# A fused attention and expert kernel: the second stage's loads asked earlier on the SP queue, the last additions in another order, the last pair in halves

## The chip, the cores and the metric

The kernel runs on one core of a Trainium2 chip. The metric is the time of one execution on the device in microseconds. Engines: PE is TensorE (matmuls), DVE is VectorE, ACT is ScalarE, POOL is GpSimd; SP is the engine that only issues DMAs here. DMAs are also issued from ACT and from POOL, each with its own queue.

## The reference

The reference computes a sparse attention and feeds its result to a mixture of experts.

- Attention: 8 batches, 8 heads, 512 local and 32 global tokens, head size 64. Global queries see all keys; local queries see the global keys and the local keys within 32 positions. Softmax in both cases. The result x has 4352 rows (8 x 544) of 512 numbers.
- Routing: `P = exp(x @ w_gate - max)` for 8 experts; then eight rounds in which the rows and then the columns are divided by their sums and everything is multiplied by N / E.
- Experts: for each of 8 experts `h = max(x @ w1[e], 0)` (512 to 1024), `y = h @ w2[e]` (1024 to 512), and `out += P[:, e] * y`.

The output is 4352 x 512 numbers in fp32.

## The kernel before

**First stage (0 to about 405 us).** Attention for all batches, the logits, and, as filling work for TensorE, the first expert layer of experts 0 to 3, whose results h are written to DRAM (`hd`). The transposed x is kept in DRAM too (`xd`), as are the fp16 copies of w1 for experts 4 to 7 (`w1d`). At the end of the stage the routing weights go to DRAM (`pd`).

**Second stage (405 to 1054 us): units and pairs.** Its work is cut into 72 units. Tokens stand in nine groups: eight of 512 local tokens, one per batch, and a last one of 256 global tokens. Each group has eight units, one per expert, in the order 4, 0, 5, 1, 6, 2, 7, 3. An even unit uses an expert of 4 to 7, whose first layer is computed here; the odd unit behind it uses an expert of 0 to 3, whose h is loaded. The loop over units (lines 922 to 961) is an order written out by hand, and every engine follows it in its own queue. A "block" here is an even unit with the odd one behind it, counted by the even unit: block 66 is units 66 and 67.

What one block i does:

- SP loads the routing weights of two units as rows spread over all partitions (`load_pb`, tile pb, 256 KB each, 128 KB in the last group), once per group the next group's x (`load_x`, tile xg), the h of unit i + 3 (`load_h`, 1 MB, 512 KB in the last group), and in the odd half the w1 of unit i + 6 (`load_w1`, tile w1s, 1 MB).
- VectorE forms the sums of unit i + 1 (`sums`, line 672 through the helper `tt`), multiplies x by the weights of unit i + 4 (`scale_x`, tile xs), multiplies the loaded h of unit i + 3 by its weights (`scale_h`), and in the odd half forms the sums of unit i + 2.
- TensorE computes the first layer of unit i + 2 (`l1`, line 734; ACT moves it out with Relu, line 736) between the products of unit i (`product`, line 777), and then the products of unit i + 1.

**The second layer in seven products.** h @ w2 is done by a scheme of Strassen's kind: seven products q = 1 to 7 of half-size blocks, from h itself (q 3, 4, 6, 7) and from the sums s (q 1, 2, 5), with weight combinations made beforehand (`prep_w2c`, done on VectorE; three of the experts are still loaded and prepared during the first blocks). Products 1 to 5 are gathered over the whole group in PSUM tiles that stay (`ps_fix`, m1 to m5). Products 6 and 7 are gathered over one block only, in tiles of a rotating PSUM pool with three buffers (`ps_rot`, tag r), which the first layer's results (ph) use as well. At a block's end `add` (lines 782 to 793) moves pm of q 6 and 7 into the output tile o; at the end of a group it also moves m1 to m5. A moved product is one or two instructions, on VectorE (line 793) or as a copy on ACT (line 791). When a group closes, `store` (line 796) issues its store on SP, 1 MB.

**Buffers.** pb, xs and xg have two buffers each, w1s two, h four. A load waits on SP until the last reader of its buffer is done. A pb takes the buffer that was freed first, so in each pair one waits for the last `scale_x` and the other for the last `scale_h`.

**The order on SP.** In the odd half: w1s, then the store if the group closes. In the next even half: pb, pb, xg if due, h. SP works through this strictly in order, so what stands behind a waiting DMA waits too.

**The end.** The last unit (71) is not done in seven products. `last_pair` (lines 798 to 817) computes the second layer of 256 tokens in two pieces of 128 rows, in a PSUM tile of 512 columns each, the right half of the columns first. VectorE adds a piece to o in one instruction (line 813), and the piece's four batches are stored by four DMAs of 64 KB, from SP, ACT and POOL. The additions of unit 70, which close the last group, are written after all its products, in the order 6, 7, 3, 4, 5, 2, 1.

Of the kernel before, what the change touches and what calls it, by code (L numbers as in the profile page):

```python
# [10 lines left out]
FP32 = mybir.dt.float32  # L11
AF = mybir.ActivationFunctionType
ALU = mybir.AluOpType
# [10 lines left out]
def kernel(  # L24
# [13 lines left out]
    nc = tc.nc  # L38
# [3 lines left out]
    D, E = moe_w_gate.shape  # L42
    F = moe_w1.shape[2]
    P = 128
# [45 lines left out]
    with tc.tile_pool(name="att_c", bufs=1) as att_c, \  # L90
# [144 lines left out]
        for a in range(2):  # L235
            r = slice(HB * a, HB * (a + 1))
# [336 lines left out]
        for s in range(HP, NU + 1):  # L573
            slot = s
            b, hp = divmod(s, HP)
# [87 lines left out]
    HF, HD = FT // 2, D // 2  # L663
# [7 lines left out]
    def tt(out, in0, in1, op):  # L671
        nc.vector.tensor_tensor(out=out, in0=in0, in1=in1, op=op)  # L672

    def prep_w2c(e):
        w = w2c[e]
        for o, a, b, op in ((0, 1, 4, ALU.add), (5, 1, 2, ALU.add), (6, 3, 4, ALU.add),
                            (2, 2, 4, ALU.subtract), (3, 3, 1, ALU.subtract)):
            tt(w[:, :, o], w[:, :, a], w[:, :, b], op)
# [8 lines left out]
    def load_w1(i):  # L687
        if i < NUN:
            w1s[i] = wpool.tile([P, DP, F], FP16, tag="w1e", name="w1s")
            nc.sync.dma_start(out=w1s[i], in_=w1d[units[i][1] - NL])  # L690

    def load_pb(i):
        if i < NUN:
            m, e = units[i]
            c0, n = groups[m]
            pbs[i] = xsp.tile([P, 512], FP32, tag="pb", name="pb")
            nc.sync.dma_start(out=pbs[i][:, 0:n], in_=pd[e, c0 : c0 + n].partition_broadcast(P))

    def load_x(m):
        if m <= B:  # L700
            xgs[m] = xsp.tile([P, DP, groups[m][1]], FP16, tag="xg", name="xg")
            nc.sync.dma_start(out=xgs[m], in_=xd[m])

    def scale_x(i):
        if i < NUN:
            m = units[i][0]
            n = groups[m][1]
            xss[i] = xsp.tile([P, DP, 512], FP16, tag="xs", name="xs")
            tt(xss[i][:, :, 0:n], xgs[m],
               pbs.pop(i)[:, 0:n].unsqueeze(1).to_broadcast([P, DP, n]), ALU.mult)  # L710

    def alloc_h(i):
        if i < NUN:
            hs[i] = hpool.tile([P, FT, groups[units[i][0]][1]], FP16, tag="hT", name="h")

    def load_h(i):
        if i < NUN:
            m, e = units[i]
            alloc_h(i)
            nc.sync.dma_start(out=hs[i], in_=hd[e][m])  # L720

    def scale_h(i):
        if i < NUN:
            n = groups[units[i][0]][1]
            h = hs[i]
            tt(h, h, pbs.pop(i)[:, 0:n].unsqueeze(1).to_broadcast([P, FT, n]), ALU.mult)

    def l1(i, fm, pool, tag):
        if i >= NUN:
            return  # L730
        n = groups[units[i][0]][1]
        ph = pool.tile([P, 512], FP32, tag=tag, name="ph")
        for dk in range(DP):
            nc.tensor.matmul(ph[:, 0:n], w1s[i][:, dk, P * fm : P * (fm + 1)], xss[i][:, dk, 0:n],  # L734
                             start=(dk == 0), stop=(dk == DP - 1))
        nc.scalar.activation(out=hs[i][:, fm, 0:n], in_=ph[:, 0:n], func=AF.Relu)  # L736

    def sums(i):
        if i >= NUN - 1:
            return  # L740
        n = groups[units[i][0]][1]
        t1, t2 = slice(0, n // 2), slice(n // 2, n)
        h = hs[i]
        s = ss[i] = (wpool.tile([P, 3, HF, 256], FP16, tag="w2e", name="s", bufs=1) if i % 2 else
                     wr.tile([P, 3, HF, 256], FP16, tag="s", name="s"))
        lo, hi = h[:, 0:HF], h[:, HF:FT]
        tt(s[:, 0:2, :, 0 : n // 2], lo[:, :, 0:n].rearrange("p k (a t) -> p a k t", a=2),
           hi[:, :, 0:n].rearrange("p k (a t) -> p a k t", a=2), ALU.add)
        tt(s[:, 2, :, 0 : n // 2], lo[:, :, t1], hi[:, :, t2], ALU.add)
        tt(lo[:, :, t2], lo[:, :, t2], lo[:, :, t1], ALU.subtract)  # L750
        tt(hi[:, :, t1], hi[:, :, t1], hi[:, :, t2], ALU.subtract)
# [5 lines left out]
    def closes(i):  # L757
        m, e = units[i]
        return e == (ORDER[-1] if m < B else ORDER[-2])
# [22 lines left out]
    def add(i, q, pm):  # L782
        m, e = units[i]
        nt = groups[m][1] // P // 2
        if m not in os_:
            os_[m] = ypool.tile([P, NJ, D], FP32, tag="y", name="o")
        for j, (r, d, sg) in enumerate(QUARTER[q]):
            o = os_[m][:, nt * r : nt * (r + 1), HD * d : HD * (d + 1)]
            p = pm[:, 0 : HD * nt].rearrange("p (t d) -> p t d", d=HD)
            if (q >= 6 and e == ORDER[1]) or (q in (3, 4) and j == 0):  # L790
                nc.scalar.mul(o, p, 1.0 / float(E))  # L791
            else:
                nc.vector.scalar_tensor_tensor(out=o, in0=p, scalar=sg / float(E), in1=o, op0=ALU.mult, op1=ALU.add)  # L793

    def store(m):
        nc.sync.dma_start(out=out[S * m + Sg : S * (m + 1)].rearrange("(c p) d -> p c d", p=P), in_=os_[m])

    def last_pair(i):
        m, e = units[i]
        o, h, w = os_[m], hs[i], w2c[e]  # L800
        n = groups[m][1]
        lo, hi = h[:, 0:HF, 0:n], h[:, HF:FT, 0:n]
        s = ss[i]
        for c in range(n // P):
            q = slice(P * c, P * (c + 1))
            pm = ps_rot.tile([P, 512], FP32, tag="r", name="pm")
            for d, terms in ((1, ((lo, 2), (s, 4))), (0, ((hi, 3), (s, 1)))):
                for t, (a, wi) in enumerate(terms):
                    for k in range(HF):
                        nc.tensor.matmul(pm[:, HD * d : HD * (d + 1)], a[:, k, q], w[:, k, wi, :],  # L810
                                         start=(d == 1 and t == 0 and k == 0),
                                         stop=(t == 1 and k == HF - 1), skip_group_check=True)
            nc.vector.scalar_tensor_tensor(out=o[:, c, :], in0=pm, scalar=1.0 / float(E), in1=o[:, c, :],  # L813
                                           op0=ALU.mult, op1=ALU.add)
            for b in range(4 * c, 4 * c + 4):
                eng = {3: nc.gpsimd, 7: nc.sync}.get(b, (nc.sync, nc.scalar)[c])
                eng.dma_start(out=out[S * b : S * b + Sg, :], in_=o[W * (b % 4) : W * (b % 4 + 1), c, :])  # L817

    fac = float(E) / float(NTOK)
# [90 lines left out]
    for fm in range(FT):  # L910
        pool, tag = cyc[fm % 2]
# [4 lines left out]
    load_w1(4)  # L916
    sums(0)
    scale_h(1)
    pss.close()
    ps_rot = ctx.enter_context(tc.tile_pool(name="ps_rot", bufs=3, space=PSUM, reuse_waits="tile"))  # L920
    ps_fix = ctx.enter_context(tc.tile_pool(name="ps_fix", bufs=1, space=PSUM, reuse_waits="tile"))
    for i, (m, e) in enumerate(units):
        if i == NUN - 1:
            last_pair(i)
        elif i % 2 == 0:
            alloc_h(i + 2)
            load_pb(i + 3)
            load_pb(i + 4)
            if (i + 4) % E == 0:
                load_x((i + 4) // E)  # L930
            load_h(i + 3)
            if i + 2 < NUN:
                sums(i + 1)
            else:
                n = groups[m][1]
                h = hs[i + 1]
                s = ss[i + 1] = wpool.tile([P, HF, n], FP16, tag="w2e", name="sl", bufs=1)
                tt(s, h[:, 0:HF, 0:n], h[:, HF:FT, 0:n], ALU.add)
            scale_x(i + 4)
            if m == 0:  # L940
                for e in {2: (2,), 4: (7,), 6: (3,)}.get(i, ()):
                    prep_w2c(e)
            scale_h(i + 3)
            for fm in range(3):
                l1(i + 2, fm, ps_rot, "r")
            for q, fm in ((3, 3), (4, 4), (5, 5), (2, 6), (1, 7), (6, None), (7, None)):
                product(i, q)
                if fm is not None:
                    l1(i + 2, fm, ps_rot, "r")
            if closes(i):  # L950
                for q in (6, 7, 3, 4, 5, 2, 1):
                    add(i, q, fixed[q])
        else:
            load_w1(i + 5)
            sums(i + 1)
            for q in (6, 7, 3, 4, 5, 2, 1):
                product(i, q)
                if q >= 6 or closes(i):
                    add(i, q, fixed[q])
            if closes(i):  # L960
                store(m)
# [31 lines left out]
```

## Time and profile before

| | |
|---|---|
| median of 3 runs | 1059.76 us (1059.38 to 1062.28) |
| the profiled execution | 1060.91 us |
| its span, first to last instruction | 1059.1 us |
| granted TensorE clock, mean | 0.996 |
| PE busy | 1024.0 us (97%) |
| DVE busy | 809.6 us (76%) |
| ACT busy | 489.1 us (46%) |
| POOL busy | 132.0 us (12%) |
| DMA | 190.82 MB, mean 180 GB/s |

A time line of the profile reads: start in us, duration in us, engine, line of the kernel, operation, what it writes and reads, the shape, how many instructions are merged into the line (x), and in brackets how long the engine stood idle before it and what ended that. SPq and ACTq are DMAs being issued on these engines. A line of waits reads: who waited (engine, tile, line), for whom, us in total, how many times, the longest. Matmuls overlap one another, so a line of x4 that says 0.60 us occupies TensorE until the next line starts. Times of single DMA packets (their size, start and landing) come from the same trace.

### The profile page before, as it was taken

The numbers are of one execution on the slowest core, as the hardware profiler recorded it, in microseconds if no ns is written. First come the engines' busy times: TensorE is split into PE (matmuls) and PEld (weight loads), VectorE is DVE, ScalarE is ACT, GpSimd is POOL, SyncE is SP. The second block draws the span as 40 slices with busy tenths as digits, with TensorE's granted clock in tenths as the row PEclk, the third lists the DMA queues.
The fourth block names the chain that finished last, engine by engine and source line by source line (L and its number), as shares of the span: only waits on it lengthen the run. The fifth ranks groups of instructions, "written<-read, shape, count | busy, mean of one in ns | idle before, by whom it ended". The sixth has DMA issues, their size and how long they took to land.

```text
span 1059.1 us, 21691 instructions
## 1 busy us (share of the span) xinstructions
PE 1024.0 (97%) x8854; PEld 698.6 (66%) x8854; DVE 809.6 (76%) x1464; ACT 489.1 (46%) x1248; POOL 132.0 (12%) x216
## 2 busy tenths in 40 slices
PE   7799999999999999999999999999999999999997
PEld 4455555555555466677777777777777777777786
DVE  8577777777775767997878777778787678668766
ACT  7678888787886674222323223223233132232231
POOL 7341423413313002000000000000000000000000
PEclk9899999999999999999999999999999999999999
DMA  9887588997946999835436346436535535436251
GB/s 267 189 208 210 106 265 195 220 241 153 255 130 177 269 283 302 246 104 189 165 139 197 123 140 199 140 120 199 170 115 177 211 97 186 180 128 181 106 176 49
DMA packets 97331, 190.82 MB, mean 180 GB/s; under 512 B 33424, under 2 KB 63584, under 8 KB 84432
## 3 DMA queue, kind: packets, MB, share of 16 engines
q1 hardware_dynamic: 54208, 159.61, 44.4%
q0 software_dynamic: 40464, 20.26, 14.7%
q10 hardware_dynamic: 2560, 9.57, 2.3%
q8 instruction: 69, 1.13, 0.4%
q14 instruction: 30, 0.25, 0.1%
HBM read 157.11 MB, written 53.62 MB: 199 GB/s over the span
## 4 chain that ended last, share of the span: by engine, by line
issue 63%; PE 21%; ACT 7%; DVE 5%; DMA 2%; POOL 1%; SPq 0%; ACTq 0%; POOLq 0%
PE ph L466 14%; ACT Pu L309 4%; DVE Pu L346 2%; ACT hT L469 1%; PE ptw L357 1%; ACT qbd L283 1%; DMA vraw<-in_v_l_dram 1%; DMA f<-in_q_l_dram 1%; DMA kgf<-in_k_g_dram 1%; PE pt L273 1%; PE ph L734 1%; PE po L378 1%; DVE m L409 1%; PE sc L299 1%; PE pt L426 1%
## 5 line engine op out<-in xcount | busy, mean ns | idle before, releaser
L736 ACT ACTIVATE h<-ph 128x512 f16<-128x512 f32 (+1 forms) x288 | 164.8, 573 | 408.4 <-PE ph L734 398.5
L734 PE MATMUL ph<-xs,w1s 128*128 128x512 f16 (+1 forms) x1152 | 269.6, 367 | 4.4 <-DVE o L793 2.9
L466 PE MATMUL ph<-xT,w1e 128*128 128x512 f16 (+1 forms) x1152 | 256.1, 367 | 0.2
L777 PEld LDWEIGHTS <-h 128*128 128x128 f16 x2160 | 211.4, 98 | 44.3
L777 PE MATMUL m<-w2c,s 128*128 128x256 f16 x1620 | 199.9, 273 | 0.0
L672 DVE TENSOR_TENSOR s<-h 128x1024 f16<-128x1024 f16 (+2 forms) x142 | 123.9, 914 | 86.3 <-PE m L777 43.3
L777 PEld LDWEIGHTS <-s 128*128 128x128 f16 x1620 | 158.5, 98 | 38.2
L734 PEld LDWEIGHTS <-w1s 128*128 128x128 f16 x1152 | 112.6, 98 | 87.6 <-issue 5.1
L466 PEld LDWEIGHTS <-w1e 128*128 128x128 f16 x1152 | 105.2, 98 | 95.8 <-issue 3.0
L672 DVE TENSOR_TENSOR h<-h,pb 128x4096 f16<-128x4096 f16 (+1 forms) x36 | 150.6, 4183 | 3.9 <-DMA h<-hd 3.4
L777 PE MATMUL m<-w2c,h 128*128 128x256 f16 x1080 | 135.2, 273 | 0.0
L469 ACT ACTIVATE hT<-ph 128x512 f16<-128x512 f32 (+1 forms) x191 | 103.6, 558 | 46.4 <-PE ph L466 45.1
L777 PE MATMUL pm<-w2c,h 128*128 128x256 f16 x1080 | 123.8, 273 | 0.0
L672 DVE TENSOR_TENSOR xs<-xg,pb 128x2048 f16<-128x2048 f16 (+1 forms) x36 | 78.1, 2169 | 53.4 <-DMA pb<-pd 47.2
L309 ACT ACTIVATE Pu<-ms,mx 128x160 f16<-128x160 f32 x224 | 93.6, 420 | 3.9 <-DVE mx L306 1.5
L471 DVE TENSOR_SCALAR hT<-ph 128x512 f16<-128x512 f32 x97 | 66.8, 688 | 31.3 <-PE ph L466 30.6
L672 DVE TENSOR_TENSOR h<-h 128x1024 f16<-128x1024 f16 (+1 forms) x142 | 87.6, 658 | 0.0
L817 POOL DMA_DIRECT2D out_dram<-o x1 | 0.5, 539 | 643.4 <-DVE o L813 643.4
L306 DVE CUSTOM_DVE_ANT_0 ms<-sc,mask 128x160 f32<-128x160 f32 x224 | 59.9, 319 | 23.2 <-PE sc L301 20.8
L350 POOL TENSOR_TENSOR Pl<-Pu,rs 128x256 f16<-128x256 f16 x32 | 24.4, 762 | 197.2 <-DVE rs L345 131.9
L346 DVE TENSOR_TENSOR Pu<-Pu,rs 128x768 f16<-128x768 f16 x64 | 45.5, 711 | 2.2
L793 DVE SCALAR_TENSOR_TENSOR o<-m,o 128x512 f32<-128x512 f32 (+1 forms) x72 | 43.2, 655 | 3.8 <-ACT o L791 2.1
(152 smaller groups left out, 934.6 us busy)
## 6 DMA issues: line engine op xcount, KB each, us to landing
w1s<-w1d SPq DMA_DIRECT2D x36, 1024.0 KB
h<-hd SPq DMA_DIRECT2D x32, 1024.0 KB
hd<-hT SPq DMA_DIRECT2D x26, 1024.0 KB
pb<-pd SPq DMA_DIRECT2D x64, 256.0 KB
w2c<-in_moe_w_dram POOLq DMA_DIRECT2D x16, 512.0 KB, 21.1
out_dram<-o SPq DMA_DIRECT2D x8, 1024.0 KB
f<-in_q_l_dram SPq DMA_DIRECT2D x15, 512.0 KB
f<-in_k_l_dram SPq DMA_DIRECT2D x15, 512.0 KB
```

The lines of the kernel that those rows point to most:

```text
L306: nc.vector.tensor_tensor_reduce(out=ms[:, ii, :], in0=sc[:, SW * ii : SW * (ii + 1)], in1=mask[:, mi, :], scale=-scale, scalar=BIG, op0=A ...
L309: nc.scalar.activation(out=d["Pu"][:, i, :], in_=ms[:, ii, :], func=AF.Exp, scale=-1.0, bias=d["mx"][:, i : i + 1], accum_out=d["sm"][:, i ...
L346: nc.vector.tensor_tensor(out=d["Pu"][:, i0:i1, 0:KW], in0=d["Pu"][:, i0:i1, 0:KW], in1=d["rs"][:, i0:i1].unsqueeze(2).to_broadcast([P, i1 ...
L350: nc.gpsimd.tensor_tensor(out=d["Pl"], in0=d["Pu"][:, :, KW:SW], in1=d["rs"].unsqueeze(2).to_broadcast([P, NHB, Sg]), op=ALU.mult)
L466: nc.tensor.matmul(ph[:, 0:n], wts[e][:, dk, P * fm : P * (fm + 1)], xT[m][:, dk, :], start=(dk == 0), stop=(dk == DP - 1))
L469: nc.scalar.activation(out=hT[:, fm, 0:n], in_=ph[:, 0:n], func=AF.Relu)
L471: nc.vector.tensor_scalar(out=hT[:, fm, 0:n], in0=ph[:, 0:n], scalar1=0.0, scalar2=None, op0=ALU.max)
L672: nc.vector.tensor_tensor(out=out, in0=in0, in1=in1, op=op)
L734: nc.tensor.matmul(ph[:, 0:n], w1s[i][:, dk, P * fm : P * (fm + 1)], xss[i][:, dk, 0:n], start=(dk == 0), stop=(dk == DP - 1))
L736: nc.scalar.activation(out=hs[i][:, fm, 0:n], in_=ph[:, 0:n], func=AF.Relu)
L777: nc.tensor.matmul(pm[:, HD * t : HD * (t + 1)], lhs[0][:, k, lhs[1] + P * t : lhs[1] + P * (t + 1)], w[:, k, q - 1, :], start=(k == 0 and ...
L793: nc.vector.scalar_tensor_tensor(out=o, in0=p, scalar=sg / float(E), in1=o, op0=ALU.mult, op1=ALU.add)
```

## The change

Three edits.

1. In the second stage, `load_pb` (both of a pair) and `load_x` are called in the odd half of the block before, in front of `load_w1`, instead of in the even half. What they load, and into which buffers, stays. The first two (units 3 and 4) are called ahead of the loop.
2. In unit 70, which closes the last group, each product is followed by its own `add`, in the order of the products: 3, 4, 5, 2, 1, 6, 7.
3. In `last_pair` each half of the columns has its own PSUM tile from the rotating pool and its own addition of 256 columns. The eight stores alternate between SP and ACT; POOL issues none.

```diff
@@ last_pair
         for c in range(n // P):
             q = slice(P * c, P * (c + 1))
-            pm = ps_rot.tile([P, 512], FP32, tag="r", name="pm")
             for d, terms in ((1, ((lo, 2), (s, 4))), (0, ((hi, 3), (s, 1)))):
+                pm = ps_rot.tile([P, HD], FP32, tag="r", name="pm")
                 for t, (a, wi) in enumerate(terms):
                     for k in range(HF):
-                        nc.tensor.matmul(pm[:, HD * d : HD * (d + 1)], a[:, k, q], w[:, k, wi, :],
-                                         start=(d == 1 and t == 0 and k == 0),
-                                         stop=(t == 1 and k == HF - 1), skip_group_check=True)
-            nc.vector.scalar_tensor_tensor(out=o[:, c, :], in0=pm, scalar=1.0 / float(E), in1=o[:, c, :],
-                                           op0=ALU.mult, op1=ALU.add)
+                        nc.tensor.matmul(pm, a[:, k, q], w[:, k, wi, :],
+                                         start=(t == 0 and k == 0), stop=(t == 1 and k == HF - 1))
+                oc = o[:, c, HD * d : HD * (d + 1)]
+                nc.vector.scalar_tensor_tensor(out=oc, in0=pm, scalar=1.0 / float(E), in1=oc, op0=ALU.mult, op1=ALU.add)
             for b in range(4 * c, 4 * c + 4):
-                eng = {3: nc.gpsimd, 7: nc.sync}.get(b, (nc.sync, nc.scalar)[c])
+                eng = (nc.sync, nc.scalar)[b % 2]
                 eng.dma_start(out=out[S * b : S * b + Sg, :], in_=o[W * (b % 4) : W * (b % 4 + 1), c, :])
@@ ahead of the loop
     scale_h(1)
+    load_pb(3)
+    load_pb(4)
     pss.close()
@@ the loop, even unit i
             alloc_h(i + 2)
-            load_pb(i + 3)
-            load_pb(i + 4)
-            if (i + 4) % E == 0:
-                load_x((i + 4) // E)
             load_h(i + 3)
...
                 product(i, q)
                 if fm is not None:
                     l1(i + 2, fm, ps_rot, "r")
-            if closes(i):
-                for q in (6, 7, 3, 4, 5, 2, 1):
+                if closes(i):
                     add(i, q, fixed[q])
@@ the loop, odd unit i
         else:
+            load_pb(i + 4)
+            load_pb(i + 5)
+            if (i + 5) % E == 0:
+                load_x((i + 5) // E)
             load_w1(i + 5)
             sums(i + 1)
```

## The prediction

> **What bounds the kernel now.** I read the page's busy times first, then TensorE's waits in the second stage (470 us to the end), then the instructions in order of time around each wait that is left, for TensorE, VectorE and the SP queue, and last the DMA packets by size.
>
> ```profile
> PE 1024.0 (97%) x8854; PEld 698.6 (66%) x8854; DVE 809.6 (76%) x1464; ACT 489.1 (46%) x1248; POOL 132.0 (12%) x216
> PE ph L734 <- DVE xs L672: 1.5, 1, 1.5
> PE ph L734 <- DVE o L793: 1.4, 1, 1.4
> DVE xs L672 <- DMA pb<-pd: 43.0, 9, 6.4
> ```
>
> TensorE is 97% busy, and after 470 us it waits twice, 2.9 us in all. VectorE waits 43.0 us in nine places for rows of weights (pb), but only one of them, in the last group, reaches TensorE. A full block of a pair takes 19.13 us of matmuls without a gap (blocks start at 521.10, 540.23, 559.37 and 578.50 us, the third of them with a pb wait of 4.56 us inside). So the second stage is a wall of matmuls; what can be won are three holes and the tail.
>
> The three holes, the last two with what VectorE and SP do there:
>
> ```profile
> 445.43 1.89 PE L734 MATMUL ph<-xs,w1s 128*128 128x512 f16 x8 [1.56 <-DVE o L793]
> 1026.42 1.47 PE L734 MATMUL ph<-xs,w1s 128*128 128x256 f16 x12 [1.50 <-DVE xs L672]
> 1036.02 0.60 PE L734 MATMUL ph<-xs,w1s 128*128 128x256 f16 x4
> 1037.99 1.03 PE L734 MATMUL ph<-xs,w1s 128*128 128x256 f16 x8 [1.37 <-DVE o L793]
> ...
> 1025.05 1.23 DVE L672 TENSOR_TENSOR xs<-xg,pb 128x1024 f16<-128x1024 f16 x1 [5.61 <-DMA pb<-pd]
> 1026.39 2.29 DVE L672 TENSOR_TENSOR h<-h,pb 128x2048 f16<-128x2048 f16 x1
> 1033.71 2.29 DVE L672 TENSOR_TENSOR h<-h,pb 128x2048 f16<-128x2048 f16 x1 [0.34 <-DMA h<-hd]
> 1037.52 0.75 DVE L793 SCALAR_TENSOR_TENSOR o<-pm,o 128x256 f32<-128x256 f32 x2
> ...
> 1017.86 0.39 SPq L796 DMA_DIRECT2D out_dram<-o  x1
> 1018.35 1.53 SPq L697 DMA_DIRECT2D pb<-pd  x2
> 1019.98 0.76 SPq L720 DMA_DIRECT2D h<-hd  x1
> 1021.02 0.32 SPq L690 DMA_DIRECT2D w1s<-w1d  x1
> 1026.30 2.73 SPq L697 DMA_DIRECT2D pb<-pd  x2
> 1029.14 1.07 SPq L720 DMA_DIRECT2D h<-hd  x1
> ```
>
> The pb of the hole at 1026.42 stands on SP behind the store of the group before, which waits for the last addition (1017.83). The hole before 1037.99 is VectorE's: it waits for h until 1033.71, runs the scaling, the sums and then the addition that frees a PSUM buffer. The tail:
>
> ```profile
> 1047.80 0.82 ACT L791 ACTIVATE o<-m 128x256 f32<-128x256 f32 x2 [3.98 <-PE m L777]
> ...
> 1049.98 0.86 DVE L793 SCALAR_TENSOR_TENSOR o<-pm,o 128x256 f32<-128x256 f32 x2 [1.93 <-PE pm L777]
> 1050.76 2.86 DVE L793 SCALAR_TENSOR_TENSOR o<-m,o 128x256 f32<-128x256 f32 x8
> 1053.54 1.28 DVE L813 SCALAR_TENSOR_TENSOR o<-pm,o 128x512 f32<-128x512 f32 x2
> ...
> 1054.85 1.40 ACTq L817 DMA_DIRECT2D out_dram<-o  x3
> ```
>
> The last matmul ends at 1053.88; VectorE ends at 1054.82 because the additions were taken up late, and ACT then issues three stores, the last from about 1055.78. The end is at 1059.1.
>
> **Part 1, the loads.** No instruction is added; TensorE's order is unchanged. On SP, each pair's two pb (and once per group the xg) pass in front of the w1s load and, where a group closes, of the store; h stays last. The first two pb (units 3 and 4) keep their place. What gates a pb is its buffer: the first of a pair waits for the xs product before it, the second for the scaling of h (SP's waits: 12.1 us for xs, 33.1 us for h). So the second pb, the w1s behind it and h now all start after that scaling.
>
> Full blocks (521.10 as example): the xs product ends at 526.54 and the scaling at 530.87, so the pair is asked at 526.6 and 530.9 instead of 532.98; w1s still waits for its matmuls (532.57). After a close the pair comes some 12 us sooner (scaling ends at 550.01, asked before at 562.57), and VectorE's waits of up to 6.4 us go. Worth on TensorE: 0, because its matmuls cover them: the example block with the 4.56 us wait is no longer than the others. w1s is needed one to two blocks later: where scaling ends late (571.98 + 4.43 = 576.4 instead of w1s at 570.83) it still has 21 us until 597.6. What is late next is h, which has w1s ahead of it wherever the scaling was later than the matmuls. In a full block both orders put the same bytes ahead of h.
>
> Hole at 445.43. VectorE works from 405 to 446 with two waits only (3.00 us for pb, 0.84 for h); up to the load of h at 413.23 the SP order is unchanged, so both stay. Then w1s goes from 416.05 to about 426.9, ahead of the h asked at 426.86. By the packets, that h was in at 435.9, and scaled from 437.42: 1.5 us of room. A w1s is 128 packets of 8 KB at 309 ns on 16 engines, 2.47 us, so h would be in at 438.4, 1.0 us late. Against that: until 436 the engines are shared with the POOL queue's w2c loads (share of the engines 1.0 to 1.24 from 411 to 439). About 450 packets of those still ran after 431.5, and at some 200 per us alone against 42 beside q1's data they gain about 490 while the w1s is away from 421 to 424. So h comes at 437.0 or a little after. I take +0.1 us, bounds -0.5 (less crowding) to +1.0.
>
> Last group. The pb for xs is there early: xs follows the sums at 1019.44 to 1020.67, and the 1.50 us hole closes; block 66 starts at 1024.92. h is asked at 1018.35 right behind the store: store data 1018.5 to 1021.7, h data 1.3 us more, in at 1023.6 (0.6 us after the last packet, as before); scaled 1023.7 to 1026.0. Now the second pb (1026.0), w1s (1026.45) and h (1026.9) follow each other. A pb asked at 1028.7 had its packets until about 1031.5, so this one until 1028.8; w1s until 1031.2; h 1.4 us more, in at 1033.2. Before it was there at 1033.7. From there the chain is the old one (scaling, sums, two additions, PSUM buffer), so the last hole ends at 1037.99 - 0.45 = 1037.54 and has grown: most of the time of the one hole moves into the other. Taken: -0.45. Bounds: -2.9 (both holes gone, if h were not held up) to +0.8 (h 0.8 us later than before).
>
> Here a rule bears. Row: a w1s asked at 570.83 and a pb at 571.87 ran strictly one after the other, 8 KB packets from 572.8 to 575.1 and the 2 KB packets after them. The Trainium skill, DMA: Bandwidth & Descriptors, section Queues, rings and completion order, says that each DMA engine takes the descriptors of one ring in order, though a later one may finish first; the trace agrees on the order. By strict order the sum is -0.45; if h overtook w1s, it would be in about 2.5 us earlier and both holes would be gone, -2.9.
>
> **Part 2, additions product by product.** The eight additions from m buffers move in front of the two from pm; the number stays ten. The first follows ACT's copy (0.41 us each from 1047.80): 1048.2 to 1048.6, the second after ACT's other copy, to 1048.98, six more at 0.357 (2.86 / 8) to 1051.12, two at 0.375 to 1051.87. All are done 1.67 us sooner than before (1053.54). But the pm buffers are freed last: q 6 at 1051.5, q 7 at 1051.87.
>
> **Part 3, the last pair in halves.** Two instructions of 0.64 us become four of 0.375 (+0.22 us of VectorE, covered), and four PSUM tiles of a pool of three replace two. The first tile is free; the second, due at 1051.09, needs q 6's buffer (1051.5), so TensorE stands 0.4 us; the third and fourth are free in time. Matmuls end at 1053.88 + 0.4 = 1054.28, the last half runs 1054.35 to 1054.73 (was 1054.82). Stores: eight as before, POOL's one goes, four each on SP and ACT; behind the last addition ACT issues two instead of three, 0.47 us less (1.40 / 3). Parts 2 and 3: -0.1 - 0.47 = -0.55. Bounds: 0 (TensorE stands as long as VectorE was late) to -1.0 (no standing).
>
> **Sum.** +0.1 - 0.45 - 0.55 = -0.9 us. The profiled execution took 1060.91 us (span 1059.1 and 1.8 around it), 1.15 above the median of 1059.76: it becomes 1060.0, and a median of **1058.9**.
>
> **Rivals.**
> - *The loads are not sooner where it counts, and the tail is eaten up* (the change does not do what it says). For it: the gates of the buffers are unchanged, and h stays last on SP. Loads 0, tail 0 to -0.3: 1059.6. Against: the store no longer stands ahead of the pb.
> - *All holes close.* h overtakes w1s, and VectorE makes up its lag: -2.9, up to -1.5 at 445, tail -1.0: 1059.76 - 5.4 = 1054.4. Against: 445 lies behind two waits that the change leaves alone.
> - *Slower: w1s stands in front of h.* It decides if h is not asked sooner than before. For the last group: if the scaling does not start before 1026.4, h is in at 1033.7 + 2.5 = 1036.2, and the last hole grows by 2.5; at 445, with no help from the w2c queue, w1s at its shared pace (3.1 us) makes h 1.6 late. +2.5 + 1.6 - 0.5 = +3.6: 1063.4. Against: the store's packets leave room for h at 1021.7.
>
> **How the numbers follow.** Forecast 0.58 (own range 1057.0 to 1060.5: the tail's bounds and half-way to those of the loads), no effect 0.18, all holes 0.11, slower 0.13. A measurement here tells 0.3%, 3.2 us, from no change: 1056.6 to 1062.9. Faster beyond that needs over half of all holes: 0.11; slower 0.12, most of its rival; the rest, 0.77, is within. The range runs from 1056.3 to 1062.2: past half of the way to either rival.
>
> **What would show it.** Right: VectorE's pb waits fall from 43 us to a few; the hole at 1026 is gone and the one behind the additions of the last group is near 2.4 us; 445.43 still waits 1.5 us; the ten additions end near 1052 and ACT issues two stores at the end. Wrong: a new wait of TensorE for w1s, or h arriving after its scaling is due in full blocks, where 11 us lie between asking and use.

## The result and the profile after

The changed kernel is slower: a ratio of 1.0035 to the kernel before, 95% interval 1.0019 to 1.0051 (medians 1064.77 us of 7 runs and 1062.14 us of 7 runs). The kernel before, known from three runs when the forecast was made, came out higher over more runs: 1062.14 here, 1061.8 (26 and 35 runs) and 1062.7 (23 runs) beside the experiments. The profiled execution of the changed kernel took 1065.27 us with a span of 1063.5 us, 4.4 us more than the span before.

Busy times, from the page of the changed kernel:

```profile
PE 1027.3 (97%) x8854; PEld 700.1 (66%) x8854; DVE 809.2 (76%) x1466; ACT 489.6 (46%) x1248; POOL 132.4 (12%) x215
```

What TensorE waited for from 400 us on, and VectorE for DMAs from 470 us on, both from the changed kernel (who, for whom, us in total, times, longest):

```profile
PE ph L734 <- DVE o L793: 6.9, 2, 4.9
PE pm L810 <- DVE o L793: 0.6, 1, 0.6
...
DVE h L672 <- DMA h<-hd: 31.9, 14, 3.7
DVE xs L672 <- DMA pb<-pd: 2.2, 1, 2.2
```

The loads did what they were moved for: VectorE's waits for pb fell from 43.0 us to 2.2. In their place stand waits for h, 2.6 us before and 31.9 now. Twelve of the 14 waits for h stand ahead of the last group, up to 3.66 us long, and none of these reaches TensorE. In the last group one does; instructions in order of time, changed kernel, TensorE, then VectorE, then SP:

```profile
447.09 1.89 PE L734 MATMUL ph<-xs,w1s 128*128 128x512 f16 x8 [2.03 <-DVE o L793]
1026.42 1.47 PE L734 MATMUL ph<-xs,w1s 128*128 128x256 f16 x12
1036.03 0.61 PE L734 MATMUL ph<-xs,w1s 128*128 128x256 f16 x4
1041.51 1.86 PE L734 MATMUL ph<-xs,w1s 128*128 128x256 f16 x8 [4.87 <-DVE o L793]
...
1025.81 2.29 DVE L672 TENSOR_TENSOR h<-h,pb 128x2048 f16<-128x2048 f16 x1 [3.57 <-DMA h<-hd]
1033.56 1.22 DVE L672 TENSOR_TENSOR xs<-xg,pb 128x1024 f16<-128x1024 f16 x1 [2.24 <-DMA pb<-pd]
1037.22 2.29 DVE L672 TENSOR_TENSOR h<-h,pb 128x2048 f16<-128x2048 f16 x1 [2.44 <-DMA h<-hd]
1041.04 0.75 DVE L793 SCALAR_TENSOR_TENSOR o<-pm,o 128x256 f32<-128x256 f32 x2
...
1019.52 0.39 SPq L796 DMA_DIRECT2D out_dram<-o  x1
1020.00 0.46 SPq L720 DMA_DIRECT2D h<-hd  x1
1022.26 6.18 SPq L697 DMA_DIRECT2D pb<-pd  x2
1028.54 0.38 SPq L690 DMA_DIRECT2D w1s<-w1d  x1
1029.01 0.38 SPq L720 DMA_DIRECT2D h<-hd  x1
```

The hole for xs at the start of block 66 is gone. The hole behind the additions grew from 1.37 to 4.87 us. On SP the second pb goes out when the scaling ends (1028.1), then w1s, then h; h is scaled from 1037.22, 8.2 us after it was asked. Before, it was asked at 1029.14 and scaled from 1033.71, 4.6 us later.

Behind the hole something new stands. Stretches of the changed kernel (from and to in us, length, busy us of each engine, then the granted TensorE clock, DMA share, GB/s):

```profile
1037.00:1041.50 4.50, 0.00 (x0) 0.00 (x0) 4.28 (x7) 0.11 (x1) 0.00 (x0) 0.92 0.34 129
1041.50:1044.50 3.00, 2.99 (x16) 2.14 (x16) 3.00 (x6) 0.77 (x2) 0.00 (x0) 0.56 0.00 0
1044.50:1048.00 3.50, 3.50 (x34) 3.14 (x33) 1.09 (x1) 1.54 (x4) 0.00 (x0) 1.00 0.00 0
```

In the 3 us after the hole the clock is 0.56 and only 16 matmuls run, against 34 in the 3.5 us after that. The kernel before, in the 3 us behind its hole of 1.37 us, ran 28 matmuls at clock 1.00:

```profile
1038.00:1041.00 3.00, 3.00 (x28) 2.69 (x28) 3.00 (x6) 1.34 (x4) 0.00 (x0) 1.00 0.00 0
```

From the hole's end to the first matmul of the last pair it is 1055.02 - 1041.51 = 13.51 us, before 1050.22 - 1037.99 = 12.23: the half clock cost 1.28 us.

The 4.4 us of span, piece by piece (after less before): first stage +1.19 (first matmul of the second stage at 398.87, before 397.68; the code there is the same), the hole near 445 us +0.47 (2.03 and 1.56), blocks in between 0.00 (567.99 us from the first product of block 4 to the start of block 64 in both), block 64 to the first matmul of the last pair +3.14 (38.21 and 35.07), last pair to the end -0.40 (8.48 and 8.88). Of the 3.14, 1.28 are the half clock and 1.85 the holes, counted between the starts of the matmuls around them: one grew by 3.51 (5.48 and 1.97), the other gave back 1.66 (1.31 and 2.97). (By the idle times in brackets the holes come to 2.00, 4.87 for 2.87, since matmuls overlap where no hole stands between them.)

### The profile page after: what moved, and what is told of

Its sections match the earlier page's. It is cut to its first block, busy times and chain, and to the rows that moved or that the text cites. A ratio compares the mean times of both kernels' runs of the same rounds, so it can differ in the third digit from the quotient of the medians.

```text
span 1063.5 us, 21725 instructions
## 1 busy us (share of the span) xinstructions
PE 1027.3 (97%) x8854; PEld 700.1 (66%) x8854; DVE 809.2 (76%) x1466; ACT 489.6 (46%) x1248; POOL 132.4 (12%) x215
## 4 chain that ended last, share of the span: by engine, by line
PE 77%; DVE 8%; ACT 7%; DMA 4%; issue 3%; SPq 0%; POOL 0%; ACTq 0%; DVEq 0%; POOLq 0%
PE m L777 26%; PE ph L734 21%; PE ph L466 14%; PE pm L777 10%; ACT Pu L309 4%; DVE Pu L346 2%; DMA h<-hd 2%; DVE h L672 2%; PE ptw L357 1%; ACT hT L469 1%; ACT qbd L283 1%; DMA vraw<-in_v_l_dram 1%; DMA f<-in_q_l_dram 1%; PE pt L273 1%; PE po L378 1%
## 5 line engine op out<-in xcount | busy, mean ns | idle before, releaser
L309 ACT ACTIVATION_READ_ACCUMULATOR Pu<-ms,mx 128x1 f32 x224 | 42.4, 189 | 0.0
```

The source lines that it names most:

```text
L309: nc.scalar.activation(out=d["Pu"][:, i, :], in_=ms[:, ii, :], func=AF.Exp, scale=-1.0, bias=d["mx"][:, i : i + 1], accum_out=d["sm"][:, i ...
```

## The experiments

The first stage's length differs from run to run by up to 4 us in these profiles, though its code is the same, so the table also gives the second stage alone: the span less the start of the first matmul at line 734 (735 where a line was added). For before that is 1059.1 - 397.68 = 661.4 us, for the changed kernel 1063.5 - 398.87 = 664.6.

| kernel | ratio to before (95%) | second stage, us | less before |
|---|---|---|---|
| changed | 1.0035 (1.0019 to 1.0051) | 664.6 | +3.2 |
| changed, again | 1.0031 (1.0015 to 1.0047) | 664.1 | +2.7 |
| tail alone | 1.0000 (0.9990 to 1.0009) | 661.3 | -0.1 |
| loads alone | 1.0026 (1.0011 to 1.0041) | 664.5 | +3.1 |
| before, one exchange | 1.0046 (1.0033 to 1.0059) | 666.7 | +5.3 |
| changed, w1s first in unit 65 | 0.9974 (0.9960 to 0.9989) | 659.1 | -2.3 |
| changed, hole filled | 1.0012 (1.0001 to 1.0024) | 662.7 | +1.3 |
| w1s behind h | 0.9990 (0.9976 to 1.0004) | 660.5 | -0.9 |
| and store behind h | 0.9977 (0.9966 to 0.9987) | 658.9 | -2.5 |
| and products 6, 7 first | 0.9970 (0.9955 to 0.9984) | 658.0 | -3.4 |
| and store last | 0.9970 (0.9956 to 0.9984) | 657.6 | -3.8 |

My theory after the result: in the last group w1s stands on SP between the second pb and the h of unit 69 and holds that h up. The rivals: the tail's edits cost the time, or the late h of unit 67 does, or the loss needs all the moved loads together.

### The two halves of the change

The tail alone is the kernel before with the edits of `last_pair` and of unit 70; its diff is the first and the fourth piece of the change's diff. The loads alone are the other pieces.

> The kernel before with the two edits of the tail alone (additions product by product, last pair in halves); the loads as before. Theory (the loss lies in the last group's loads: w1s stands between the second pb and the h of unit 69): 0.4 us below before, as the stretch from the first matmul of the last pair to the end went from 8.88 to 8.48 us; two holes of 1.5 and 1.4 us in the last group stay. Rival (the tail's edits cost it: four PSUM tiles in three buffers hold TensorE up): 2 us or more above before.

> The changed kernel with the tail of before; only the loads are moved. Theory: 0.4 us above the changed kernel, so 3 to 5 us above before, with one hole of over 4 us in the last group and the half clock behind it. Rival: within 1 us of before.

The tail alone is the same time as before within 0.1%; the loads alone are 0.26% slower, 2.8 us, just under the 3 to 5 forecast. Loads alone, TensorE in the last group:

```profile
1042.29 1.86 PE L734 MATMUL ph<-xs,w1s 128*128 128x256 f16 x8 [4.35 <-DVE o L793]
```

The loads carry the loss, and the first rival falls. The 0.4 us of the tail can be read in the profile (last pair to the end 1060.1 - 1051.59 = 8.5 us, 8.88 before), but the interval of 1 us either way does not show it as time. The tail-alone kernel's wait in the last pair:

```profile
1053.22 0.60 PE L810 MATMUL pm<-w2c,h 128*128 128x256 f16 x4 [0.59 <-DVE o L793]
```

### One exchange on SP, both ways

The kernel before with the pair of pb ahead of one w1s load, that of unit 70:

```diff
         else:
+            if i == NUN - 7:
+                load_pb(i + 4)
+                load_pb(i + 5)
             load_w1(i + 5)
...
             alloc_h(i + 2)
-            load_pb(i + 3)
-            load_pb(i + 4)
+            if i != NUN - 6:
+                load_pb(i + 3)
+                load_pb(i + 4)
```

> The kernel before with one exchange on SP: in unit 65 the two pb of units 69 and 70 pass in front of the w1s load. Everything else as before. Theory: this alone holds the h of unit 69 up by some 3 us, makes the hole behind the additions of the last group over 4 us long with the half clock behind it, and gives 3.5 to 5 us above before. Rival (the loss needs all the moved loads together, one exchange is covered): within 1 us of before.

The changed kernel with that w1s load ahead of the pair again:

```diff
         else:
+            if i == NUN - 7:
+                load_w1(i + 5)
             load_pb(i + 4)
             load_pb(i + 5)
             if (i + 5) % E == 0:
                 load_x((i + 5) // E)
-            load_w1(i + 5)
+            if i != NUN - 7:
+                load_w1(i + 5)
```

> The changed kernel, but in unit 65 alone the w1s load stands in front of the two pb again. Theory: the h of unit 69 has no w1s ahead of it and is in at about 1033.5 instead of 1037.2 us; the hole of 4.87 us shrinks to 1 to 2 us, no half clock, some 5 us below the changed kernel and 0 to 1.5 us below before. Rival (the h of unit 67, late behind a store that took 4 us, is what counts): the hole stays above 4 us and the time within 1 us of the changed kernel.

One exchange makes the kernel before 0.46% slower; the exchange taken back makes the changed kernel 0.26% faster than before. Before with the exchange, TensorE, VectorE and SP:

```profile
1039.87 1.87 PE L734 MATMUL ph<-xs,w1s 128*128 128x256 f16 x8 [3.76 <-DVE o L793]
...
1035.58 2.29 DVE L672 TENSOR_TENSOR h<-h,pb 128x2048 f16<-128x2048 f16 x1 [3.08 <-DMA h<-hd]
...
1025.78 2.67 SPq L697 DMA_DIRECT2D pb<-pd  x2
1028.54 0.94 SPq L690 DMA_DIRECT2D w1s<-w1d  x1
1029.58 0.37 SPq L720 DMA_DIRECT2D h<-hd  x1
```

The changed kernel with the exchange taken back, VectorE and TensorE:

```profile
1027.16 2.29 DVE L672 TENSOR_TENSOR h<-h,pb 128x2048 f16<-128x2048 f16 x1 [3.59 <-DMA h<-hd]
1034.30 2.29 DVE L672 TENSOR_TENSOR h<-h,pb 128x2048 f16<-128x2048 f16 x1 [0.49 <-DMA h<-hd]
...
1038.59 1.03 PE L734 MATMUL ph<-xs,w1s 128*128 128x256 f16 x8 [0.63 <-DVE o L793]
```

The theory holds in both directions. The first run agrees with its forecast of 3.5 to 5 us (4.9 by the ratio) in part by luck: h was scaled only 1.9 us later than before (1035.58 and 1033.71), not 3, and the hole was 3.76 us, not over 4; but the clock stayed at half for 6.83 us, so that hole's end to last pair took 1055.01 - 1039.87 = 15.14 us, 2.91 more than before. The h of unit 67 is as late here as in the changed kernel (a wait of 3.59 us), and the hole is 0.63 us all the same: that rival falls too. I had expected 0 to 1.5 us below before and got 2.8, since the second hole shrank further than I thought.

### Is it the idle time that halves the clock?

```diff
+        for rpt in range(9 if (i == NUN - 2 and fm == 0) else 1):
+            for dk in range(DP):
-        for dk in range(DP):
-            nc.tensor.matmul(ph[:, 0:n], ...)
+                nc.tensor.matmul(ph[:, 0:n], ...)
```

> The changed kernel with the four matmuls of one first-layer tile of unit 70, the one ahead of the hole, done nine times over (the same result nine times), 3.5 us of matmuls inside the hole of 4.87 us. If the half clock (0.56 from 1041.5 to 1044.5 us) comes from TensorE standing idle: the hole's end stays, the clock stays full, 1.3 us below the changed kernel. If the half clock comes on its own: the same time as the changed kernel, within 0.5 us, and a half clock at the same place.

The matmuls in the hole, and the stretches around it:

```profile
1034.17 4.09 PE L735 MATMUL ph<-xs,w1s 128*128 128x256 f16 x36
1039.11 1.03 PE L735 MATMUL ph<-xs,w1s 128*128 128x256 f16 x8 [0.85 <-DVE o L794]
...
1034.00:1038.20 4.20, 4.20 (x40) 3.65 (x38) 3.37 (x4) 0.00 (x0) 0.00 (x0) 1.00 0.42 148
1038.20:1039.10 0.90, 0.06 (x1) 0.00 (x0) 0.90 (x4) 0.38 (x1) 0.00 (x0) 1.00 0.00 0
1039.10:1042.00 2.90, 2.89 (x27) 2.59 (x27) 2.90 (x6) 1.22 (x4) 0.00 (x0) 1.00 0.02 6
```

VectorE is no earlier for it, and TensorE still waits for it; but the clock stays at 1.00, and from the hole's end to the first matmul of the last pair it is 1051.34 - 1039.11 = 12.23 us, as before the change. Work without use in the hole wins back 1.28 us. The second stage is 1.9 us shorter than the changed kernel's; the rest is a hole that happened to be 0.5 us shorter (first matmul of the unit to the second tile 4.94 us, 5.48 in the changed kernel).

### Loads behind h

w1s behind h everywhere:

```diff
             load_h(i + 3)
+            if i > 0:
+                load_w1(i + 4)
...
-            load_w1(i + 5)
             sums(i + 1)
```

> The changed kernel with every w1s load asked behind the h of the same block instead of in front of the store and h. Theory (what hurts is w1s ahead of h): VectorE's waits for h fall from 31.9 us to under 15, the hole of the last group to under 2 us, the time like that of the run with the single w1s put back, 2 to 3 us below before. Rival (w1s then comes too late): TensorE waits for w1s in the last group, where the first layer of unit 70 starts some 9 us after the load is asked.

VectorE's waits for h did not fall (28.3 us, most of them behind the stores), and w1s now came too late once. TensorE's waits, this kernel:

```profile
PE ph L734 <- DVE o L793: 2.2, 2, 1.8
PE ph L734 <- DMA w1s<-w1d: 1.7, 1, 1.7
PE pm L810 <- DVE o L793: 0.6, 1, 0.6
```

The hole of the last group is down to 0.43 us, as the theory says, but the w1s of unit 68, now behind the store, costs 1.7 us: a part of each side was right. The time, 0.9990, is not told from before.

The store behind h as well (from the closing odd unit to the next even one):

```diff
             load_h(i + 3)
+            if i > 0 and i % E == 0:
+                store(m - 1)
             if i > 0:
                 load_w1(i + 4)
...
-            if closes(i):
-                store(m)
```

> The run before this one with the store of a closed group also behind the h, so that h waits for no addition. Theory: the h of unit 67 is in before its scaling is due, the scalings of the last group follow one another without a wait, and both holes of the last group are gone: a further 0.5 to 1.5 us below, 3 to 4 us below before. Rival: the buffer of h, freed late by the products of the unit before, sets when h can be asked; the time stays as in the run before.

VectorE then waits for no h at all after 470 us, and both holes of the last group are gone but for 0.5 us of w1s: 0.9977, 2.4 us below before by the ratio, less than the 3 to 4 expected. Then products 6 and 7 of unit 70 first:

```diff
-            for q, fm in ((3, 3), (4, 4), (5, 5), (2, 6), (1, 7), (6, None), (7, None)):
+            for q, fm in (((6, None), (7, None), (3, 3), (4, 4), (5, 5), (2, 6), (1, 7)) if closes(i) else
+                          ((3, 3), (4, 4), (5, 5), (2, 6), (1, 7), (6, None), (7, None))):
```

> As the run before, with products 6 and 7 of unit 70 done and added first instead of last, so that their PSUM buffers are free when the last pair asks for them. Theory: TensorE's wait of 0.59 us in the last pair goes, the stretch from its first matmul to the end falls by 0.6 us, a further 0.3 to 0.6 us below. Rival: the waits behind products 3 to 1 move to the last addition and nothing is won.

The wait in the last pair is gone, and its first matmul to the end is 1056.5 - 1048.79 = 7.7 us (8.5 in the run before). By their times the two cannot be told apart (0.9977 and 0.9970, intervals overlapping). Last, the store behind w1s too, and the changed kernel once more on the same chip as that run:

> The run with products 6 and 7 first, with the store of a closed group behind w1s as well, so last on SP. Theory: the w1s of unit 68, which then waits for no addition either, is in before its block starts and TensorE's last wait in the last group (0.5 us) goes; holes left: the one near 445 us of about 1.8 us. 0.3 to 0.8 us below the run with the store ahead of w1s, so 3 to 4.5 us below before. Rival: the 0.5 us comes back behind another load, no difference.

> The changed kernel itself once more, on the chip of the run above. Theory: 3 to 5 us above before, one hole of 4 to 5 us in the last group with the half clock behind it. Rival (the first measurement of it was a matter of its chip): within 1 us of before.

With the store last, TensorE waits once after 400 us:

```profile
PE ph L734 <- DVE o L793: 2.0, 1, 2.0
```

That is the hole near 445 us. The ratio is 0.9970 again: the step itself is not told from the run before it, but by the ratios the kernel is 3.2 us below before, and the changed kernel beside it 3.3 us above.

## Why the prediction was wrong

**Which part failed.** I forecast -0.9 us with a range to 1062.2; the measured 1064.77 lies above it. The case that came is the rival "w1s stands in front of h", which I had given 0.13 and a time of 1063.4.

**Full blocks and closings: right.** Worth 0; measured 0.00 us over 568 us. VectorE's pb waits fell to a few us, as forecast. But what I had named as a sign of being wrong, h arriving after its scaling is due in full blocks, came too: twelve waits for h between 490 and 970 us. They cost TensorE nothing, so the sign was ill chosen.

**The hole near 445 us.** Forecast +0.1, bounds -0.5 to +1.0. The changed kernel's profiles show 2.03 and 1.80, before 1.56; but two kernels with before's loads there (tail alone and the one exchange) show 1.93 and 1.77. No effect is shown.

**The last group: the wrong term.** Forecast -0.45, measured +3.14. The failing step is the time of the second pb: "A pb asked at 1028.7 had its packets until about 1031.5, so this one until 1028.8", 2.8 us from asking to the last packet. In the changed kernel it was asked at 1028.13 and its last packet ended at 1033.18, 5.05 us later. The steps behind it were sized nearly right. In the changed kernel's time, which is 1.66 us later there, the forecast had pb until 1030.5, w1s until 1032.9 and h in at 1034.9. The last landings came at 1033.53 for pb, at 1035.98 for w1s, 2.45 us behind it, and at 1037.20 for h, another 1.22 us behind; h was scaled from 1037.22, 2.3 us after the forecast. Only about 0.5 us of that came from asking late (1028.13 instead of 1026.0 + 1.66 = 1027.7, as the h of unit 67 was scaled from 1025.81 instead of 1025.4). The 2.3 us and the half clock of 1.28 us, which the forecast did not have, make up the 3.6 us between -0.45 and +3.14.

Each of these loads lands in 16 parts, one for each DMA engine. Those of the pb are spread from 1030.46 to 1033.53, those of w1s from 1033.91 to 1035.98, those of h from 1035.15 to 1037.20, and h is done when the last part is. The Trainium skill, DMA: Bandwidth & Descriptors, Why a DMA increments its semaphore by 16 and not by 1, says that the engines of one DMA finish independently and that only the full 16 means that all has landed; the trace agrees, with 3.1 us between the first and the last for the 128 KB of pb. Which engine a packet ran on is not in the trace. That the engines late with pb were the ones late with w1s and h is inferred from the spacing: the last eight landings of w1s come 2.4 to 2.8 us behind the last eight of pb, near the 2.47 us of packets that w1s takes on an engine, and those of h 1.2 us behind these. So the order on the queue held as forecast, although its row was read a little short (17 of the 128 packets of that w1s ran from 571.8 us).

Why that pb was slow stays open. From asking to the last landing it took 5.4 us in the changed kernel, 4.7 in its second profile, 4.2 with the loads alone and 4.3 with the hole filled; but 3.4 before, 3.1 with the one exchange and 3.0 with the exchange taken back.

**The rival's condition was off as well.** I had said that it decides only if h is not asked sooner than before. It was asked sooner (1029.01, less 1.66, against 1029.14), and the rival came all the same, since the pb took longer. That a slow pb is not needed is shown by the run with the single exchange: there the pb took 3.1 us, and h was still scaled 6.0 us after it was asked (1029.58 to 1035.58), against 4.6 before. The order on SP alone does it.

**The cost that no case had.** I forecast a hole of 2.4 us and priced it by its length. At 4.87 it halved the clock behind it, 1.28 us more.

**The tail.** Forecast -0.55; the profiles show -0.40. As forecast, the ten additions ended early (1056.92 us, 1052.1 when counted as in the profile before) and ACT issued two stores behind the last addition. That the two numbers are so near is partly luck, as two errors cancel. TensorE stood 0.59 us in the last pair (forecast 0.4), and counted from the first matmul of the last pair VectorE ended 0.26 us later than before (4.86 and 4.60 us), not 0.1 sooner; from there to the end it took 0.66 us less (3.62 and 4.28), where 0.47 was forecast. The runs cannot tell the tail from 0.

**The base.** The forecast stood on a median of three runs, 1059.76; the kernel before has a median near 1062 over more runs, and single runs from 1057.15 to 1065.27. With the base right the middle would have been 1061.2: 2.4 of the 5.9 us between forecast and measured time are the base's. The rest stays: 0.9 us sooner was forecast, and by the ratio it came 3.7 us later.

## What to carry to other kernels

When a load is moved ahead in a queue that is worked through in order, price what it is moved in front of for each stage by itself: here the same move cost nothing in eight groups of full blocks, where mostly 11 us lie between asking for h and scaling it, and 3 us in the last, where the blocks are half as long. Put first what is used first: behind pb, the order h, w1s, store won 0.3% (in a kernel that also does products 6 and 7 first, which by itself was not told from nothing), where w1s, store, h lost 0.35%. And an estimate of a transfer must start from the last landing of what stands ahead of it in the same queue: here a row spread over all partitions (128 KB) took 3.0 to 5.4 us to land, and the loads behind it kept its delay.

## What the runs showed of the hardware

- Idle TensorE for long enough and the clock behind it is halved. In the second stage, holes of up to 2.03 us left it at 1.00; holes of 3.76, 4.35, 4.49 and 4.87 us each had half clock behind them, for 3.41 us in three of them and 6.83 us with the one of 3.76. In the changed kernel it fell at 1040.76 us, 4.1 us into the hole. With the hole filled by repeated matmuls it stayed at 1.00. No run here has a hole between 2.03 and 3.76 us. The Trainium skill, TensorE: Matmul & The Clock Gate, Part 1: The HAM clock gate, gives an idle window of about 3.4 us after which the clock drops to half, on a window that runs freely. The trace agrees: half clock came in pieces of once or twice 3.41 us, and in the changed kernel the clock's fall at 1040.76 us lies 986.45 us, 289 times 3.413, behind its last change before.
- The first stage's length varies from run to run: the first matmul of the second stage came between 396.40 and 400.23 us in twelve profiles of the same first-stage code. Half-clock stretches of 3.41 or 6.83 us lie near 8, 34 and 51 us, one of them in the profile before, two in those of the changed kernel, three in the run with one w1s put back. The stage goes with their sum: 397.5 us on average in the four profiles with 6.83 us of half clock there, 398.9 in the seven with 10.24, 400.23 in the one with 13.65. But within the seven it runs from 397.16 to 400.23, and TensorE's wait there for a tile that POOL writes (vsr) differs too, from 1.0 to 5.3 us. How much of the spread is the clock's was not tried.
